# Pooled attention and two MLPs on one core: k's and v's rows loaded two tiles to a transfer, a batch's transfers ahead of its sums

## The chip, the core and the metric

The kernel runs on one core of one Trainium2 chip. A core has TensorE (PE: matrix products, with the loading of its stationary operand shown as PEld), VectorE (DVE), ScalarE (ACT), GpSimd (POOL), and SyncE (SP), whose queue here issues nearly all transfers; 16 DMA engines move the data. Each engine works through a queue of its own in the order of the program and waits at semaphores for the others. The metric is the device time of one execution in microseconds. Lower is better.

## What is computed

```python
def attn(q, k, v):            # (8, 8, 576, 64) each: batch, head, token, dim
    k_p = k.reshape(B, H, 72, 8, D).mean(axis=3)      # 72 pooled keys
    v_p = v.reshape(B, H, 72, 8, D).mean(axis=3)
    s = (q @ k_p.transpose(0, 1, 3, 2)) / sqrt(D)
    e = exp(s - s.max(-1)); return (e / e.sum(-1)) @ v_p
x = attn(q, k, v)             # as (4608, 512)
x = ((x @ w1) * (x @ w2)) @ w3 @ w_out                # w1, w2: 512 x 1024
out = relu(x @ w_in) ** 2 @ w_out2                    # 512 -> 2048 -> 512
```

## The kernel before

Every float32 operand of a large product is kept as two words, hi (ScalarE casts it) and lo (VectorE subtracts; `split`, L119 and L120), and a product is three matmuls: hi hi, hi lo, lo hi (`mm3`). In what follows, the cut of a tile is the VectorE instruction that makes its lo word. A matmul of 512 columns takes about 0.23 us.

The first 110 us are the start-up: `fold` multiplies w3 into w_out (L778), with the attention of the first tokens between. Then the 4608 tokens run as nine blocks of 512. A block has eight steps of `stage_ab` (24 matmuls ps_w, from x and w1 and w2; their product is gf, and its words are gt) and of `stage_w` (12 matmuls acc, from gt). The weights of half of these steps are fetched in units of 128x512 (`fetch`, L225, tile un, a ring of eight), each after TensorE has used the unit whose place it takes. After the nine blocks the second MLP runs over pairs of blocks with seven products in place of eight (`h_step`, L1088; `o_step`, L1190), the last block alone.

The attention that yields the next tokens is cut into tasks, and so is the preparation of the second MLP's weights ("quarters": tiles rq or raw, wq, sq, oq, stores u_A, u_S, u_oA, u_oS). Both are spread through the matmuls by `tick`, which `run_mm` calls after every six matmuls. Attention's tasks for a half of a batch's tokens are: the transposes of the pooled keys (ps_kt, copied to kbd), the scores (ps_s), their maxima on VectorE (mx, L467), the exponentials on ScalarE (att, L470) and sums (sm), transposes (ps_t; copied as aT, and the remainder as aR), four products with v (ps_av, first with aT, then with aR), and the casts and cuts that make x (L531, L534).

The pooling is the part that is changed. `kv_parts` loads a batch's k as five tiles (four of 128 rows, one of 64; every row is eight tokens of 64) and v as four tiles and a remainder ("odd", two transfers of 16 rows), 256 KB for a full tile, into the pool raw_p. The pool has three places, which it shares with the quarters' tiles rq and raw and later x2r. VectorE sums each tile over the eight tokens (`total`, L314, into kp or vp; the remainder of v, L311); v is then cut into vl and vr (L348). For every batch but the first, `load_back` takes one part from a list at each tick: part j sums tile j - 2 and issues the load of tile j. While a quarter is held between its loading and its conversion (`held`), no part is taken unless more than nine are left. The first batch's loads all go out at the beginning but for the last of v's tiles and the remainder, which a task of their own loads.

The operands of the next pair of blocks (`operands_of`: one load and seven cuts; x2r, x2o) are made in the steps h and o of the pair before it, at places that are written out by hand.

Of the kernel before, what the change touches and what calls it, by code (L numbers as in the profile page):

```python
# [35 lines left out]
def attn_moe_moe2_kernel(  # L36
# [242 lines left out]
    def load_back():  # L279
        if back["kv"] and not wait_kv[0] and (not held[0] or len(back["kv"]) > 9):  # L280
            back["kv"].pop(0)[1]()
        if back["q"] and ticks[0] % 2 == 0 and not (keep_q[0] and len(back["q"]) % Q_PARTS == 0):
            back["q"].pop(0)[1]()
# [3 lines left out]
    def kv_parts(src, b, dst, last):  # L287
# [4 lines left out]
        def load(j):  # L292
            pool, tag = (raw_p, "raw") if b else (wW_p, "w")
            if src is v and j == NP:
                raws[j] = r = pool.tile([RB, 2, POOL, D], F32, tag=tag, name="kv")
# [6 lines left out]
            raws[j] = r = pool.tile([P, POOL, D], F32, tag=tag, name="kv")  # L302
            if src is k:
                n = kv_rows(j)
                nc.sync.dma_start(r[:n], flat[j * P:j * P + n])
            else:
                nc.sync.dma_start(r, flat[j * 2 * SP:j * 2 * SP + P])

        def total(j):
            if src is v and j == NP:  # L310
                nc.vector.reduce_sum(v5, raws[j].rearrange("p a r d -> p a d r"), axis=AX.X)  # L311
                return
            n = kv_rows(j)
            nc.vector.reduce_sum(  # L314
                dst(j)[:n], raws[j][:n].rearrange("p r d -> p d r"), axis=AX.X)

        def part(j):
            if j >= 2:
                total(j - 2)
            if j < NJ:  # L320
                load(j)

        if b == 0:
            fits = NJ if src is k else U1 - NJ
            for j in range(fits):
                load(j)
            rest = [lambda: [load(j) for j in range(fits, NJ)]]
            return rest + [(lambda j=j: total(j)) for j in range(NJ)] + last
        parts = [(lambda j=j: part(j)) for j in range(NJ + 2)] + last
# [1077 lines left out]
    for step in order:  # L1407
        if step[0] == "h":
# [7 lines left out]
            if u == 0 and n == 0:  # L1416
                assert not todo_x
                head = False
            if u == NU - 1 and n in (1, 3, 4, 5, 6) and todo_x:
                todo_x.pop(0)()  # L1420
                head = n == 6
        elif step[0] == "ph":
            ph_step(*step[1:])
            prepare()
        else:
# [8 lines left out]
            if todo_x and head and step[2:] in ((0, 2), (0, 5), (1, 1), (1, 3)):  # L1434
# [36 lines left out]
```

## Time and profile before

| What | Value |
|---|---|
| time, median of 3 runs | 1528.61 us (1528.12 to 1530.61) |
| the profiled execution | 1530.13 us, of which the span shown is 1528.4 |
| TensorE busy | 1489.2 us, 97% of the span |
| VectorE, ScalarE busy | 997.0 us (65%), 797.2 us (52%) |
| mean granted clock of TensorE | 0.996 |
| transfers of k and v in full tiles | 32 each, 256 KB |

TensorE's busy share is the first thing to read: at 97% some 39 us are left in which it stands idle. About half of them lie in the start-up. The time of a whole run is a little longer than the span of the profile, which goes from the first to the last instruction.

### The profile page before, as it was taken

The page shows a single profiled execution, that of the slowest core. Times are in us where ns is not written, and L with a number is a line of the kernel's source. Part 1 is how long each engine was busy: PE and PEld are TensorE (multiplying, and loading weights), DVE is VectorE, ACT ScalarE, POOL GpSimd, SP SyncE. Part 2 cuts the span into 40 slices and gives each one's busy share as a digit, 9 for nine tenths or more (in the row PEclk, how much of TensorE's full clock was granted, in tenths as well). Part 3 has the DMA queues.
Part 4 walks back from the last instruction along what each step waited for, and adds up shares of the span by engine and source line. Part 5 has one row for each costly group of instructions (what it writes and reads, how often), then busy time and mean ns, then how long its engine had stood idle before and what let it go on. Part 6 is the DMA issues. An engine that isn't in the chain of part 4 may idle for free.

```text
span 1528.4 us, 21325 instructions
## 1 busy us (share of the span) xinstructions
PE 1489.2 (97%) x6752; PEld 1198.1 (78%) x6752; DVE 997.0 (65%) x1798; ACT 797.2 (52%) x1953; POOL 84.0 (5%) x144
## 2 busy tenths in 40 slices
PE   6899999999999999999999999999999999999998
PEld 3457778787888888878888878888888888888887
DVE  7998676757676368783255476759675967576542
ACT  6966464545545345563144574457445744464441
POOL 1011111111110011110000000000000000000000
PEclk9999999999999999999999999999999999999999
DMA  9555565757587257693339777777777867788752
GB/s 303 182 162 159 150 199 142 225 133 222 148 238 210 82 145 228 194 296 115 108 127 306 216 208 227 208 208 231 234 207 207 232 207 207 206 270 282 210 161 91
DMA packets 292783, 301.34 MB, mean 197 GB/s; under 512 B 119360, under 2 KB 184896, under 8 KB 292672
## 3 DMA queue, kind: packets, MB, share of 16 engines
q1 hardware_dynamic: 287488, 290.54, 65.3%
q10 hardware_dynamic: 5184, 9.44, 1.7%
q8 instruction: 55, 0.90, 0.3%
q14 instruction: 56, 0.46, 0.1%
HBM read 243.27 MB, written 56.62 MB: 196 GB/s over the span
## 4 chain that ended last, share of the span: by engine, by line
PE 70%; DVE 5%; ACT 3%; DMA 2%; issue 1%; SPq 0%; ACTq 0%; DVEq 0%
PE o L1190 18%; PE ps_w L185 17%; PE acc L185 8%; PE ps_a L1088 5%; PE ps_c L1088 5%; PE ps_d L1088 5%; PE ps_h L185 3%; PE o L185 3%; PE ps_b L1088 3%; PE ps_s L453 1%; PE ps_av L185 1%; ACT att L470 1%; DVE gt L120 1%; DVE x2o L120 1%; PE ps_t L500 1%
## 5 line engine op out<-in xcount | busy, mean ns | idle before, releaser
L1190 PE MATMUL o<-gt,un 128*128 128x512 f32 x1344 | 329.9, 390 | 1.4 <-DVE gt L120 1.0
L1190 PEld LDWEIGHTS o<-gt,un 128*128 128x128 f32 x1344 | 251.7, 188 | 56.0 <-DVE gt L120 3.5
L120 DVE TENSOR_TENSOR gt<-gs,gt 128x512 fp32r<-128x512 f32 x240 | 164.7, 688 | 182.9 <-ACT gt L119 181.5
L185 PE MATMUL ps_w<-x,wt 128*128 128x512 f32 x960 | 244.4, 400 | 4.4 <-ACT x L531 2.6
L119 ACT CAST gt<-gs 128x512 fp32r<-128x512 f32 x240 | 148.6, 620 | 154.7 <-PE o L1190 88.7
L185 PE MATMUL acc<-gt,Wt 128*128 128x512 f32 x864 | 215.9, 395 | 0.0
L185 PEld LDWEIGHTS ps_w<-x,wt 128*128 128x128 f32 x960 | 176.9, 190 | 44.0 <-DVE x L534 5.4
L185 PEld LDWEIGHTS acc<-gt,Wt 128*128 128x128 f32 x864 | 160.2, 188 | 32.3 <-issue 0.2
L185 PE MATMUL ps_w<-x,un 128*128 128x512 f32 x768 | 184.2, 392 | 0.0
L185 PEld LDWEIGHTS ps_w<-x,un 128*128 128x128 f32 x768 | 142.6, 188 | 29.6 <-issue 0.4
L470 ACT ACTIVATE att<-ps_s,mx 128x72 f32<-128x72 f32 (+1 forms) x320 | 97.8, 323 | 47.2 <-DVE mx L468 46.0
L1095 ACT ACTIVATE r<-r 128x512 f32<-128x512 f32 x96 | 60.7, 632 | 118.1 <-DVE r L1125 117.6
L815 DVE TENSOR_TENSOR gf<-asb,ps_w 128x512 f32<-128x512 f32 x72 | 49.3, 685 | 92.3 <-PE ps_w L185 85.4
L1088 PE MATMUL ps_a<-x2o,un 128*128 128x512 f32 x384 | 97.9, 389 | 0.2 <-ACT p L1113 0.2
L1088 PE MATMUL ps_c<-x2o,un 128*128 128x512 f32 x384 | 97.6, 389 | 0.0
L1088 PE MATMUL ps_d<-x2o,un 128*128 128x512 f32 x384 | 97.4, 389 | 0.0
L1096 ACT ACTIVATE gs<-r 128x512 f32<-128x512 f32 x144 | 90.0, 629 | 2.3 <-DMA x2r<-x2d 0.6
L1164 DVE TENSOR_TENSOR gs<-gs 128x512 f32<-128x512 f32 x128 | 86.6, 684 | 0.0
L119 ACT CAST gt<-gf 128x512 fp32r<-128x512 f32 x72 | 44.7, 621 | 79.2 <-DVE gf L815 79.2
L811 ACT COPY asb<-ps_w 128x512 f32<-128x512 f32 x72 | 42.3, 588 | 82.4 <-PE ps_w L185 82.0
L1088 PEld LDWEIGHTS ps_a<-x2o,un 128*128 128x128 f32 x384 | 72.0, 188 | 15.5 <-ACT p L1113 0.6
L1088 PEld LDWEIGHTS ps_c<-x2o,un 128*128 128x128 f32 x384 | 72.0, 188 | 15.2 <-DVE u L1119 0.3
(113 smaller groups left out, 1996.5 us busy)
## 6 DMA issues: line engine op xcount, KB each, us to landing
un<-u_w SPq DMA_DIRECT2D x128, 256.0 KB, 3.3
un<-u_A SPq DMA_DIRECT2D x128, 256.0 KB, 3.0
un<-u_S SPq DMA_DIRECT2D x128, 256.0 KB, 3.0
un<-u_oS SPq DMA_DIRECT2D x128, 256.0 KB, 3.0
un<-u_oA SPq DMA_DIRECT2D x96, 256.0 KB, 3.0
raw<-in_moe_w_dram SPq DMA_DIRECT2D x32, 512.0 KB, 5.4
raw<-in_moe_w_out_dram SPq DMA_DIRECT2D x24, 512.0 KB, 5.5
kv<-in_k_dram SPq DMA_DIRECT2D x32, 256.0 KB, 3.4
```

The source lines that it names most:

```text
L119: nc.scalar.copy(hi, src)
L120: return (eng or nc.vector).tensor_sub(lo, src, f32(hi))
L185: (lambda a=a, b=b, i=i: nc.tensor.matmul(ps, a, b, start=first and i == 0, stop=last and i == n - 1))
L453: nc.tensor.matmul(ps[:n, x * 2 * SP:(x + 1) * 2 * SP], t[:, hp, c0:c0 + n], kbd[:, hp].rearrange("p a s -> p (a s)"), start=True, stop=True)
L470: nc.scalar.activation(av[:, h0 + h], sv[:, h], ACTF.Exp, bias=mx[:n, h:h + 1], scale=scale, accum_out=sm[:n, h0 + h:h0 + h + 1])
L811: nc.scalar.copy(asb, ps)
L815: nc.vector.tensor_mul(gf, asb, pss[1])
L1088: nc.tensor.matmul(ps, l, r, start=first and j == 0, stop=j == len(todo) - 1, skip_group_check=True)
L1095: nc.scalar.activation(t, src, ACTF.Relu)
L1096: nc.scalar.activation(take(name), t, ACTF.Square)
L1164: d = nc.vector.tensor_sub(src, a, src)
L1190: nc.tensor.matmul(ob[x][o], l, r, start=u == 0 and m != 5 and j == 0, stop=u == NU - 1 and j == 2, skip_group_check=True)
```

## The change

k's and v's tiles are loaded two to a transfer: tiles 0 and 1, tiles 2 and 3, then the last one (or v's remainder). In the list of parts a batch's three loads come first, at three successive ticks, and then the sums, one to a tick: a tile that was summed two ticks after its load is now summed three to five ticks after it. The threshold of a held quarter goes from nine to ten parts. In the first batch k is loaded as before, and v's loads, remainder and all, are issued at the beginning; the two tasks that loaded the rest are gone. For the first pair of blocks, the cuts of the next pair's operands are taken at three places of the last h steps in place of five, at three o steps, and one in the next pair's second h step.

```diff
@@ -277,7 +277,7 @@
             back[name].pop(0)[1]()
 
     def load_back():
-        if back["kv"] and not wait_kv[0] and (not held[0] or len(back["kv"]) > 9):
+        if back["kv"] and not wait_kv[0] and (not held[0] or len(back["kv"]) > 10):
             back["kv"].pop(0)[1]()
         if back["q"] and ticks[0] % 2 == 0 and not (keep_q[0] and len(back["q"]) % Q_PARTS == 0):
             back["q"].pop(0)[1]()
@@ -289,44 +289,40 @@
         flat = src[b].rearrange("h (s r) d -> (h s) r d", r=POOL)
         raws = {}
 
-        def load(j):
-            pool, tag = (raw_p, "raw") if b else (wW_p, "w")
-            if src is v and j == NP:
-                raws[j] = r = pool.tile([RB, 2, POOL, D], F32, tag=tag, name="kv")
+        pool, tag = (raw_p, "raw") if b else (wW_p, "w")
+        groups = [[j] for j in range(NJ)] if src is k and b == 0 else [[0, 1], [2, 3], [4]]
+
+        def load(js):
+            if src is v and js == [NP]:
+                r = pool.tile([RB, 2, POOL, D], F32, tag=tag, name="kv")
+                raws[NP] = r.rearrange("p a r d -> p a d r")
                 odd = flat.rearrange("(a b s) r d -> b s a (r d)", a=2, b=2)
                 for x in range(2):
                     nc.sync.dma_start(
                         r[x * RM:(x + 1) * RM].rearrange("p a r d -> p a (r d)"),
                         odd[x, P:2 * SP])
                 return
-            raws[j] = r = pool.tile([P, POOL, D], F32, tag=tag, name="kv")
-            if src is k:
-                n = kv_rows(j)
-                nc.sync.dma_start(r[:n], flat[j * P:j * P + n])
-            else:
-                nc.sync.dma_start(r, flat[j * 2 * SP:j * 2 * SP + P])
+            m = len(js)
+            j0, n = js[0], kv_rows(js[0])
+            r = pool.tile([P, m, POOL, D], F32, tag=tag, name="kv")
+            rows_of = flat[j0 * P:j0 * P + n * m].rearrange(
+                "(j p) r d -> p j (r d)", j=m) if src is k else flat.rearrange(
+                    "(j w) r d -> w j (r d)", w=2 * SP)[:P, j0:j0 + m]
+            nc.sync.dma_start(r[:n].rearrange("p j r d -> p j (r d)"), rows_of)
+            for x, j in enumerate(js):
+                raws[j] = r[:n, x].rearrange("p r d -> p d r")
 
         def total(j):
-            if src is v and j == NP:
-                nc.vector.reduce_sum(v5, raws[j].rearrange("p a r d -> p a d r"), axis=AX.X)
-                return
             n = kv_rows(j)
             nc.vector.reduce_sum(
-                dst(j)[:n], raws[j][:n].rearrange("p r d -> p d r"), axis=AX.X)
-
-        def part(j):
-            if j >= 2:
-                total(j - 2)
-            if j < NJ:
-                load(j)
-
+                v5 if src is v and j == NP else dst(j)[:n], raws[j], axis=AX.X)
+
+        totals = [(lambda j=j: total(j)) for j in range(NJ)] + last
         if b == 0:
-            fits = NJ if src is k else U1 - NJ
-            for j in range(fits):
-                load(j)
-            rest = [lambda: [load(j) for j in range(fits, NJ)]]
-            return rest + [(lambda j=j: total(j)) for j in range(NJ)] + last
-        parts = [(lambda j=j: part(j)) for j in range(NJ + 2)] + last
+            for js in groups:
+                load(js)
+            return totals
+        parts = [(lambda js=js: load(js)) for js in groups] + totals
         what = (src is k, b)
         back["kv"].extend((what, fn) for fn in parts)
 
@@ -1414,11 +1410,14 @@
                 todo_x = operands_of(nxt) if nxt < len(pairs) else plain_operands()
                 todo_x.pop(0)()
             if u == 0 and n == 0:
-                assert not todo_x
+                assert len(todo_x) <= (p == 1)
                 head = False
-            if u == NU - 1 and n in (1, 3, 4, 5, 6) and todo_x:
+            if u == NU - 1 and n in ((1, 4, 6) if p == 0 else (1, 3, 4, 5, 6)) and todo_x:
                 todo_x.pop(0)()
                 head = n == 6
+            if p == 1 and u == 0 and n == 1:
+                todo_x.pop(0)()
+                assert not todo_x
         elif step[0] == "ph":
             ph_step(*step[1:])
             prepare()
@@ -1431,7 +1430,8 @@
                     sums_o.insert(0, t.rearrange("p x c -> p (x c)"))
             prepare()
             n_out += 1
-            if todo_x and head and step[2:] in ((0, 2), (0, 5), (1, 1), (1, 3)):
+            if todo_x and head and step[2:] in (
+                    ((0, 2), (0, 5), (1, 1)) if step[1] == 0 else ((0, 2), (0, 5), (1, 1), (1, 3))):
                 todo_x.pop(0)()
             (o_step if step[0] == "o" else po_step)(*step[1:])
     for p in reversed(late):
```

What stands in the queues before and now, at two places. In a row stand the line, the operation, and out<-in by the program's names. Tile numbers count differently in the two programs, and lines of the changed kernel are up to four lower (L467 is L463, L534 is L530) or, for the sums, L317.

VectorE in block 1, before: from v's fourth sum (vp) to the remainder's sum (v_99).

```order
L314 TENSOR_REDUCE vp<-kv 128x64
L467 TENSOR_REDUCE mx<-ps_s 128x4 x2
L468 TENSOR_SCALAR mx<-mx 128x4
L348 SCALAR_TENSOR_TENSOR vl<-vp,rows,vl 128x4x64
L468 TENSOR_SCALAR mx<-mx 128x4
L348 SCALAR_TENSOR_TENSOR vl<-vp,rows,vl 128x4x64
L815 TENSOR_TENSOR gf<-asb,ps_w_2073 128x512
L888 TENSOR_TENSOR sq<-wq,sq 128x256
L311 TENSOR_REDUCE v_99<-kv 32x128
L476 TENSOR_SCALAR sm<-sm 128x8
L120 TENSOR_TENSOR gt<-gf,gt 128x512
```

And now, from v's second sum to the maxima mx of the same scores:

```order
L317 TENSOR_REDUCE vp<-kv 128x64
L504 TENSOR_TENSOR aR<-ps_t,aR 32x2x128
L317 TENSOR_REDUCE vp<-kv 128x64 x2
L317 TENSOR_REDUCE v_99<-kv 32x128
L344 SCALAR_TENSOR_TENSOR vl<-vp,rows,vl 128x4x64 x2
L344 SCALAR_TENSOR_TENSOR vr<-v_99,rows,vr 32x2x64
L883 TENSOR_TENSOR sq<-wq 128x256
L463 TENSOR_REDUCE mx<-ps_s 128x4 x2
L464 TENSOR_SCALAR mx<-mx 128x4
L344 SCALAR_TENSOR_TENSOR vr<-v_99,rows,vr 32x2x64
L464 TENSOR_SCALAR mx<-mx 128x4
```

The remainder's sum and the cuts vl and vr stand ahead of the two maxima now; they stood behind them. TensorE at the same place, before, from the scores ps_s whose maxima these are:

```order
L453 MATMUL ps_s<-kbd,qT 128x144 x4
L185 MATMUL ps_w_2073<-x_2_883,wt 128x512 x3
L185 MATMUL ps_w_2073<-x_3_908,wt 128x512 x3
L185 MATMUL acc_1318<-gt,Wt 128x512 x3
L185 MATMUL acc_1319<-gt,Wt 128x512 x3
L500 MATMUL ps_t<-ident,att_105 128x128 x4
L185 MATMUL acc_1320<-gt,Wt 128x512
L505 MATMUL ps_t<-ident,rem 96x128 x2
```

And now:

```order
L449 MATMUL ps_s<-kbd,qT 128x144 x4
L185 MATMUL ps_w_2048<-x_2_861,wt 128x512 x3
L185 MATMUL ps_w_2048<-x_3_878,wt 128x512 x3
L185 MATMUL acc_1335<-gt,Wt 128x512 x3
L185 MATMUL acc_1336<-gt,Wt 128x512 x3
L185 MATMUL acc_1337<-gt,Wt 128x512 x3
L185 MATMUL acc_1338<-gt,Wt 128x512 x3
L496 MATMUL ps_t<-ident,att_105 128x128 x4
L501 MATMUL ps_t<-ident,rem 96x128 x2
```

The transposes ps_t stand behind twelve acc matmuls now, and stood behind six.

VectorE at the start of block 3, before:

```order
L815 TENSOR_TENSOR gf<-asb,ps_w_3611 128x512
L120 TENSOR_TENSOR gt<-gf,gt 128x512
L902 TENSOR_TENSOR oq<-sq,oq 128x512
L508 TENSOR_TENSOR aR<-ps_t,aR 32x2x64
L467 TENSOR_REDUCE mx<-ps_s 128x4
L468 TENSOR_SCALAR mx<-mx 128x4
L534 TENSOR_TENSOR x_0_2809<-ps_av,x_0_2809 128x64
L534 TENSOR_TENSOR x_0_3687<-ps_av,x_0_3687 128x256
L467 TENSOR_REDUCE mx<-ps_s 128x4
L314 TENSOR_REDUCE vp<-kv 128x64
```

And now:

```order
L811 TENSOR_TENSOR gf<-asb,ps_w_3545 128x512
L472 TENSOR_SCALAR sm<-sm 128x8
L473 RECIPROCAL sm<-sm 128x8
L120 TENSOR_TENSOR gt<-gf,gt 128x512
L317 TENSOR_REDUCE vp<-kv 128x64 x2
L504 TENSOR_TENSOR aR<-ps_t,aR 32x2x64
L463 TENSOR_REDUCE mx<-ps_s 128x4
L464 TENSOR_SCALAR mx<-mx 128x4
L317 TENSOR_REDUCE vp<-kv 128x64 x2
L530 TENSOR_TENSOR x_0_2772<-ps_av,x_0_2772 128x64
```

Two sums of v stand ahead of aR, and two more ahead of the first cut of x; none stood ahead of either. SyncE ahead of that, before, from the second of four unit fetches to the first loads of v:

```order
L225 DMA un<-u_w_5_1_1499 128x512
L209 DMA u_A_3_3223<-oq 128x2x128
L209 DMA u_A_2_3225<-oq 128x2x128
L209 DMA u_A_3_3227<-oq 128x2x128
L225 DMA un<-u_w_5_0_1375 128x512
L209 DMA u_A_2_3269<-oq 128x2x128
L225 DMA un<-u_w_5_1_1537 128x512
L209 DMA u_A_3_3271<-oq 128x2x128
L209 DMA u_A_2_3273<-oq 128x2x128
L209 DMA u_A_3_3275<-oq 128x2x128
L307 DMA kv<-in_v_dram 128x512 x3
```

And now, from two stores ahead of the second fetch to the last of v's loads:

```order
L209 DMA u_A_3_3279<-oq 128x2x128
L209 DMA u_A_2_3281<-oq 128x2x128
L225 DMA un<-u_w_5_1_1497 128x512
L209 DMA u_A_3_3283<-oq 128x2x128
L225 DMA un<-u_w_5_0_1377 128x512
L311 DMA kv<-in_v_dram 128x2x512
L225 DMA un<-u_w_5_1_1548 128x512
L311 DMA kv<-in_v_dram 128x2x512
L301 DMA kv<-in_v_dram 16x2x512 x2
```

v's first load stands behind the third fetch of the four now; it stood behind the fourth and three stores more.

## Rows read from the trace of the kernel before

**Rows 1.** Waits of TensorE: line, releaser, total, times, longest, in us.

```profile
PE ps_w L185 <- ACT x L531: 2.6, 1, 2.6
...
PE ps_t L500 <- DVE gf L815: 2.2, 1, 2.2
...
PE ps_w L185 <- DVE x L534: 1.7, 1, 1.7
...
PE o L1190 <- DVE gt L120: 1.0, 1, 1.0
```

**Rows 2.** Windows: length, busy PE, PEld, DVE, ACT, POOL, granted clock, DMA share, GB/s.

```profile
212.00:216.00 4.00, 2.28 (x11) 1.85 (x12) 4.00 (x8) 4.00 (x20) 0.00 (x0) 0.91 0.89 268
216.00:220.00 4.00, 4.00 (x13) 3.10 (x13) 1.25 (x4) 1.26 (x3) 1.62 (x3) 0.67 0.89 285
283.00:287.00 4.00, 3.77 (x16) 2.61 (x17) 3.88 (x11) 1.40 (x4) 1.15 (x1) 1.00 0.79 247
```

**Rows 3.** Timeline of TensorE in block 1: start, busy, instruction.

```profile
209.61 1.54 PE L185 MATMUL acc<-gt,Wt 128*128 128x512 f32 x6
213.37 0.63 PE L500 MATMUL ps_t<-ident,att 128*128 128x128 f32 x4 [2.22 <-DVE gf L815]
```

**Rows 4.** Timeline of VectorE in block 1.

```profile
198.98 0.46 DVE L467 TENSOR_REDUCE mx<-ps_s 128x4 f32<-128x288 f32 x1 [0.77 <-PE ps_s L453]
...
210.94 0.82 DVE L467 TENSOR_REDUCE mx<-ps_s 128x4 f32<-128x288 f32 x2
```

**Rows 5.** Groups of VectorE, 199 to 210.9: busy and mean.

```profile
L314 DVE TENSOR_REDUCE vp<-kv 128x64 f32<-128x512 f32 x4 | 4.1, 1056 | 0.0
L902 DVE TENSOR_TENSOR oq<-wq,oq 128x512 fp32r<-128x512 f32 x2 | 2.3, 1161 | 0.0
```

**Rows 6.** Window 199 to 211, VectorE's instructions on the tile rq alone.

```profile
199.00:211.00 12.00, 1.81 (x3) 1.00 0.57 175
```

**Rows 7.** Timeline of VectorE in the start-up.

```profile
27.43 0.17 DVE L476 TENSOR_SCALAR sm<-sm 128x8 f32<-128x8 f32 x1 [2.58 <-ACT att L470]
...
49.21 1.91 DVE L311 TENSOR_REDUCE v<-kv 32x128 f32<-32x1024 f32 x1
...
51.65 0.86 DVE L348 SCALAR_TENSOR_TENSOR vl<-vp,rows,vl 128x256 fp32r<-128x256 f32 x2
```

**Rows 8.** DMA view: issues, count, KB each, median us to landing.

```profile
raw<-in_moe_w_out_dram SPq DMA_DIRECT2D x24, 512.0 KB, 5.5
...
kv<-in_v_dram SPq DMA_DIRECT2D x32, 256.0 KB, 4.0
...
x2r<-x2d SPq DMA_DIRECT2D x2, 512.0 KB, 4.8
```

**Rows 9.** All transfers of the tile kv.

```profile
DMA to landing us min/median/max: 2.1/3.4/8.6
```

**Rows 10.** Timeline of TensorE at the start of block 2.

```profile
268.24 5.60 PE L185 MATMUL ps_w<-x,un 128*128 128x512 f32 x24
...
277.00 0.66 PE L453 MATMUL ps_s<-kbd,qT 128*128 128x144 f32 x4
```

**Rows 11.** Timeline of VectorE there.

```profile
273.95 0.69 DVE L815 TENSOR_TENSOR gf<-asb,ps_w 128x512 f32<-128x512 f32 x1 [2.12 <-PE ps_w L185]
```

**Rows 12.** Timeline of TensorE at the start of block 3.

```profile
353.71 3.04 PE L185 MATMUL ps_w<-x,un 128*128 128x512 f32 x12
...
361.03 0.30 PE L518 MATMUL ps_av<-aR,vr 96*128 96x320 f32 x1
```

**Rows 13.** Timeline of VectorE there.

```profile
358.75 0.69 DVE L120 TENSOR_TENSOR gt<-gf,gt 128x512 fp32r<-128x512 f32 x1 [0.69 <-ACT gt L119]
```

**Rows 14.** Timeline of SyncE there.

```profile
355.90 0.42 SPq L225 DMA_DIRECT2D un<-u_w  x1
```

**Rows 15.** Timeline of ScalarE in block 7.

```profile
677.27 0.62 ACT L898 CAST oq<-sq 128x512 fp32r<-128x512 f32 x1 [1.88 <-DMA u_oA<-oq]
```

**Rows 16.** Timeline of VectorE in the last half-steps of the first pair.

```profile
903.44 1.90 DVE L120 TENSOR_TENSOR x2o<-x2r,x2o 128x512 fp32r<-128x512 f32 x3
```

## The prediction

> **What bounds the kernel now.** I read the waits of TensorE first: it is busy 97% of the span, so little but its own gaps can change the time. After the start-up only four gaps exceed half a microsecond: 2.6, 2.2, 1.7 and 1.0 us, each once [rows 1]. Before them stands the start-up (folding w3 into w_out), whose idle time is spread over many short waits.
>
> A gap costs more than its length. After the 2.2 us gap the granted clock is 0.91 in the stretch of the gap and 0.67 in the next: between the chip's two levels, 2.4 GHz (1.00) and 1.2 GHz (0.50). After the 1.7 us gap it stayed at 1.00 [rows 2]. I take the loss behind a long gap as (1 - 0.67) x 4 us = 1.3, plus some of the 0.36 of the stretch before: 1.5 us.
>
> So the change is worth what it does to these gaps, less the gaps that it opens. It lives on VectorE's queue, which works in the order of the program: a sum of v that stands there and waits for its transfer holds every cut behind it.
>
> **Block 1 (the 2.2 us gap).** The reader sees TensorE end its acc matmuls at 211.1 and wait for ps_t until 213.37 [rows 3]. What it lacks are exponentials whose maxima VectorE took only at 210.94, after working without a pause from 198.98 [rows 4]: 2.4 us from the maxima to ps_t. In the new order three conversions of rq stand earlier and leave this stretch (1.81 us, [rows 6]) and so does one cut oq (1.16, [rows 5]): 3.0 us. The remainder of v (1.91) comes in, with two cuts vl (0.86) and a smaller one, vr (my estimate 0.3) [rows 7]: 3.1 us. The maxima stay at about 210.9, ps_t at 213.3. But TensorE now has twelve acc matmuls ahead of ps_t, not six: 1.5 us more work [rows 3], so it arrives at 212.5 and waits 0.8 to 0.9. Gain 2.2 - 0.9 = 1.3, and without the fall of the clock 1.5 more: **-2.8**. Bounds: 0 (the wait stays) and -3.7 (it goes).
>
> **Block 2 (the 1.7 us gap).** New: the first pair of v tiles is issued one unit fetch and one store into the 24 matmuls that begin at 268.24. A fetch waits for six matmuls, a quarter of 5.60: 269.6; two issues at 0.4 [rows 14] put the transfer at 270.5 [rows 10]. How long 512 KB of k or v take, no row shows. The nearest rows: 4.0 for 256 KB of v, 4.8 and 5.5 for 512 KB of other tensors [rows 8]; 3.4 is the median of kv's own transfers and 8.6 their longest [rows 9]. I take 4.8, the row of like size whose 512 KB stand alone; bounds 3.4 and 8.6. It lands at 275.3. VectorE is there at 274.6, after gf [rows 11], and now has the two sums (1.06 each, [rows 5]) ahead of gt: 277.4; gt 278.1, a third sum 279.1, x's cut 279.5. TensorE reaches the matmul that needs this cut after ps_s (277.00 and 0.5) and three more at 0.23: 278.4 [rows 10]. It waits 1.1 in place of 1.7: **-0.5**. At 3.4 the wait is 0.5 (-1.2); at 8.6 it is 4.9 and the clock falls (+4.7).
>
> **Block 3 (no gap now).** The same move opens one. Now aR's cut follows oq, and the sums come much later. New: two sums stand ahead of aR. The transfer follows the third fetch, which needs the first six of twelve matmuls from 353.71: 355.2 [rows 12], issued at 355.6 (as late as 356.3 if the fetch comes at 355.90 as now, [rows 14]); landing 360.4. VectorE is free at 359.4 [rows 13], waits, sums until 362.5, cuts aR at 362.8. TensorE now reaches aR's matmul at 361.03 [rows 12]; four more acc matmuls stand ahead of it, so 361.9. Wait 0.9. Then two more sums stand ahead of x's cut: maxima until 363.4, sums until 365.5, cut 365.8, against TensorE's arrival at 365.1 (five acc's, ps_s and one matmul after aR): 0.7. Behind these two cuts TensorE's next acc and ps_w matmuls are queued, and no other engine. **+1.6**, no fall of the clock since each gap is under 1.7. At 3.4: aR is in time and only the 0.7 is left (+0.7); at 8.6: 4.7 + 0.7 + 1.5 = +6.9.
>
> At one place a rule and the rows differ. The rows give 4.8 and 5.5 for 512 KB [rows 8]. The Trainium skill (DMA: Bandwidth & Descriptors, section Anatomy of one DMA) gives a transfer a fixed 2.0 us and its bytes at 436 GB/s, fitted on another issuing path; my estimate by that page is 3.2 us for 512 KB, and the sum would be that of the third case below. No transfer of 512 KB in these rows is so fast.
>
> **The other parts.** Sums of k go four in one piece in block 2; TensorE's ps_s waits a little for the copy behind them: **+0.2** (0 to 0.8). Blocks 4 to 6: the maxima stand ahead of the sums in the new order, and TensorE has twelve or more ps_w matmuls of an older block to fill: 0, as it is now; without that fill they would cost what block 3 does. Block 7 (2.6 us): x's cast waits behind an oq cast that a store's landing released [rows 15]. Its quarter runs one step earlier now, but two wq conversions come ahead of the cast: **-0.3** (-4 to +1).
>
> The first pair: three operand cuts stand before gt (1.90 us for three, [rows 16]). In the new order three instructions fewer precede the same gt, 1.9 us, more than the 1.0 of the gap: **-1.0** (0 to -1.0). The cuts themselves move behind the gt's, under o matmuls that do not wait for them.
>
> The start-up: all of v's first sums now come in one go, before the first aT. That is one sum, the remainder and three cuts moved ahead: 1.06 + 1.91 + 0.86 + 0.6 = 4.4 us [rows 5, 7], into a place where VectorE sat idle for 2.58 [rows 7]. The work behind it is 1.8 late, but 4.4 us go from the middle of the fold, where TensorE waits for the same engine. Bounded by -2.6 (the idle time is all won) and +1.8 (only the delay counts); I take **-1.0**. DMA issues become fewer everywhere: of k five per batch become three, of v six become four.
>
> **The sum.** -2.8 - 0.5 + 1.6 + 0.2 - 0.3 - 1.0 - 1.0 = -3.8. The profiled execution took 1530.1 us, 1.5 more than the median of the runs (1528.61): 1526.3 for such an execution, 1524.8 for the median.
>
> **Rivals.**
> First, slower: the pairs of transfers land late. Both go out back to back, 1 MB beside fetches and stores; 8.6 us has been seen [rows 9]. Block 3's sums then hold aR. At a landing of 8 us: block 2 +4.1, block 3 +6.3, sum +5.5, 1534.1. It decides from 6.8 us on (sum above +3). Against it: 4.8 and 5.5 for like sizes.
> Second, no change: block 1's wait stays, since VectorE still takes the maxima last. Then the first term is 0, the sum -1.0, 1527.6. For it: the maxima do not move in my own count.
> Third, faster than forecast: transfers issued earlier are landed when their sums come. At 3.4 us block 2 gives -1.2, block 3 +0.7, k 0: sum -5.6, 1523.0. For it: 3.4 is kv's median. This is the case of the Trainium skill's advice (the same page, Rules for kernel authors) to issue a transfer early and wait for it late.
>
> **Chances.** Forecast 0.38 (its own range 1522.5 to 1527), third 0.20, second 0.24, first 0.18. A measurement of this kernel tells about 0.2%, 3.06 us, from no change. Of the forecast's 0.38, 0.25 lie beyond that: faster 0.25 + 0.20 = 0.45; same 0.13 + 0.23 = 0.36; slower 0.19. The range 1520.5 to 1533 leaves out the farther halves of the first and third cases.
>
> **What would show it.** Right: ps_t's wait in block 1 below 1.2 us and the clock at 1.00 behind it; waits near 1 us on x's cut in block 2 and on aR and x in block 3; the gap before o gone; 512 KB of kv landing in 4 to 5.5 us. Wrong: a wait above 2 us with a lower clock at block 3, the 2.2 us wait of block 1 unmoved, or a start-up that ends over 2 us earlier or later than now, since its order on TensorE changes at many places and I have counted only VectorE's.

## The result and the profile after

The change made the kernel slower: 1538.93 us (1535.36 to 1540.09, 6 runs) against 1528.36 us of before on the same chip (1526.96 to 1531.37, 6 runs), a ratio of 1.0058 [1.0046, 1.0071]. Forecast were 1524.8 us, within 1520.5 to 1533, and a small gain. A second set of runs on another chip, below, gave 1.0036. The profiled execution after took 1535.36 us, its span 1533.6. It is the fastest of the six: its span is 5.2 us longer than that of before, while 0.58% are 8.9 us. Where the other 3.7 go, no trace here shows.

The waits of TensorE after, the answer to [rows 1] (line, releaser, total, times, longest, in us):

```profile
PE ps_t L496 <- issue: 4.3, 5, 1.3
PE ps_w L185 <- ACT x L527: 3.4, 2, 2.1
PE ps_t L501 <- DVE aT L120: 3.2, 2, 1.9
PE ps_w L774 <- DVE wo L155: 2.9, 2, 2.4
...
PE ps_av L185 <- DVE x L530: 2.4, 1, 2.4
PE ps_w L185 <- DVE x L530: 1.6, 2, 1.0
PE ps_s L449 <- ACT att L466: 1.5, 1, 1.5
...
PE ps_av L185 <- DVE aR L504: 0.8, 1, 0.8
```

The gaps of 2.2 and 1.0 us are gone, those of 2.6 and 1.7 are 2.1 and 1.0. But others have come: 2.4 (on wo), 2.4 (on x) and 1.9 us (on aT) in the start-up, 1.5 in block 0, 1.3 and 0.8 in later blocks.

**The start-up.** TensorE after, from the transposes of the second aT (start, busy, instruction):

```profile
30.84 0.63 PE L501 MATMUL ps_t<-ident,rem 128*96 128x128 f32 x2 [1.88 <-DVE aT L120]
31.26 2.85 PE L399 MATMUL ps_q<-ident,q_nat 128*128 128x128 f32 x12
34.17 2.29 PE L449 MATMUL ps_s<-kbd,qT 128*128 128x144 f32 x8
38.91 8.07 PE L774 MATMUL ps_w<-wo,w3t 128*128 128x512 f32 x12 [2.44 <-DVE wo L155]
```

And before, where the twelve matmuls of the fold stood ahead of the scores ps_s:

```profile
31.41 6.86 PE L778 MATMUL ps_w<-wo,w3t 128*128 128x512 f32 x12 [0.41 <-DVE wo L155]
...
38.54 0.90 PE L453 MATMUL ps_s<-kbd,qT 128*128 128x144 f32 x6
```

VectorE after, at that place: it sits idle until the scores come, and the steps that make wo follow their maxima.

```profile
35.54 0.46 DVE L463 TENSOR_REDUCE mx<-ps_s 128x4 f32<-128x288 f32 x1 [2.71 <-PE ps_s L449]
36.50 0.46 DVE L463 TENSOR_REDUCE mx<-ps_s 128x4 f32<-128x288 f32 x1 [0.50 <-PE ps_s L449]
36.87 0.42 DVE L152 TENSOR_SCALAR raw<-raw 128x512 uint32<-128x512 uint32 x1
```

In the windows after (columns as in [rows 2]) the clock stays at its lower level nearly throughout:

```profile
30.00:33.00 3.00, 2.11 (x9) 1.73 (x10) 1.95 (x5) 2.79 (x12) 1.40 (x3) 0.61 1.03 412
33.00:36.00 3.00, 2.94 (x14) 2.42 (x13) 0.46 (x1) 2.65 (x6) 0.22 (x2) 0.50 0.29 116
36.00:39.00 3.00, 0.56 (x3) 0.24 (x2) 2.47 (x7) 2.25 (x8) 0.00 (x0) 0.50 0.01 3
39.00:42.00 3.00, 3.00 (x4) 1.38 (x5) 2.86 (x6) 3.00 (x12) 0.00 (x0) 0.50 0.64 188
42.00:45.00 3.00, 3.00 (x5) 1.14 (x4) 2.93 (x7) 1.93 (x7) 0.00 (x0) 0.61 0.73 203
```

Before, two of these windows were below 1.00:

```profile
30.00:33.00 3.00, 2.60 (x10) 1.53 (x11) 2.90 (x5) 3.00 (x7) 0.00 (x0) 0.66 0.46 164
33.00:36.00 3.00, 3.00 (x7) 1.25 (x6) 2.97 (x7) 2.80 (x5) 0.00 (x0) 0.77 0.83 264
```

A window's time at 1.2 GHz is 2 x (1 - clock) x its length: 13.7 us after, 3.4 before. It fell behind waits of 0.9 and 1.9 us between 27.5 and 30.9 us, and the gap of 2.44 lies in the middle of it.

From the fold's first product to its last, before and after:

```profile
15.36:111.67 96.31, 83.92 (x311) 44.54 (x311) 90.38 (x177) 74.23 (x206) 11.19 (x17) 0.98 0.66 207
```

```profile
16.77:116.60 99.83, 87.92 (x315) 48.32 (x316) 88.46 (x178) 75.94 (x214) 10.66 (x17) 0.91 0.66 200
```

TensorE is idle for 12.4 us of this stretch before and 11.9 after, so its waits have not grown in sum; the 3.5 us more are time in which it is busy, at a clock of 0.91 in place of 0.98.

**The blocks.** TensorE after, at the places of the prediction (block 1, 2, 3) and at two more:

```profile
215.34 2.90 PE L185 MATMUL acc<-gt,Wt 128*128 128x512 f32 x12
219.50 0.63 PE L496 MATMUL ps_t<-ident,att 128*128 128x128 f32 x4 [1.25 <-issue]
220.71 0.39 PE L501 MATMUL ps_t<-ident,rem 128*96 128x128 f32 x2 [0.58 <-issue]
...
283.64 0.50 PE L185 MATMUL ps_w<-x,wt 128*128 128x512 f32 x1 [1.04 <-DVE x L530]
...
364.87 0.70 PE L185 MATMUL ps_av<-aT,vl 128*128 128x320 f32 x3 [0.83 <-DVE aR L504]
...
606.31 2.62 PE L185 MATMUL ps_w<-x,wt 128*128 128x512 f32 x9 [1.29 <-ACT x L527]
...
907.09 16.48 PE L1186 MATMUL o<-gt,un 128*128 128x512 f32 x72
```

Block 1: twelve acc matmuls stand ahead of ps_t and the wait is 1.25 in place of 2.2 [rows 3]; the granted clock from 216 to 220 us is 1.00. Blocks 2 and 3: waits of 1.04 and 0.83. At 907 the o matmuls run without a gap.

**Where the time went.** Waits hide each other, so I also took from each profile the start of fixed matmuls: the fold's first product, the 1st and the 145th acc matmul (the second is in block 1), the first and the last o matmul. In the last column stands the span:

| kernel | fold's first | first acc | 145th acc | first o | last o | span |
|---|---|---|---|---|---|---|
| before | 15.4 | 134.4 | 265.4 | 900.3 | 1479.8 | 1528.4 |
| after | 16.8 | 141.1 | 267.5 | 907.1 | 1485.2 | 1533.6 |
| after minus before | +1.4 | +6.6 | +2.1 | +6.8 | +5.4 | +5.2 |

From the fold's first product to the first acc 5.2 us are lost (3.5 up to the fold's last product, 1.7 behind it, in block 0), block 1 gives 4.5 back, blocks 2 to 8 lose 4.7, the first pair gives back 1.4. The first 1.4 us, ahead of the fold, are no work of the change: the kernels that leave the first batch alone vary there from 15.4 to 17.4.

### The profile page after: what moved, and what is told of

Read it like the earlier page. It is cut to its first block, busy times and chain, and to the rows that moved or that the text cites. A ratio compares the mean times of both kernels' runs of the same rounds, so it can differ in the third digit from the quotient of the medians.

```text
span 1533.6 us, 21274 instructions
## 1 busy us (share of the span) xinstructions
PE 1490.1 (97%) x6752; PEld 1201.4 (78%) x6752; DVE 994.3 (65%) x1798; ACT 798.6 (52%) x1953; POOL 83.3 (5%) x144
## 4 chain that ended last, share of the span: by engine, by line
PE 83%; DVE 7%; DMA 4%; ACT 3%; issue 2%; SPq 1%; DVEq 0%; ACTq 0%
PE ps_w L185 22%; PE o L1186 18%; PE acc L185 11%; PE ps_c L1084 5%; PE ps_a L1084 5%; PE ps_d L1084 5%; PE ps_h L185 3%; PE o L185 3%; PE ps_b L1084 3%; PE ps_s L449 2%; PE ps_w L774 2%; PE ps_av L185 1%; DMA raw<-in_moe_w_out_dram 1%; DMA raw<-in_moe_w_dram 1%; PE ps_t L496 1%
## 5 line engine op out<-in xcount | busy, mean ns | idle before, releaser
L811 DVE TENSOR_TENSOR gf<-asb,ps_w 128x512 f32<-128x512 f32 x72 | 49.3, 684 | 99.6 <-PE ps_w L185 94.5
L1084 PEld LDWEIGHTS ps_d<-x2o,un 128*128 128x128 f32 x384 | 72.1, 188 | 15.0
```

Of the source, the lines that this page charges most:

```text
L811: nc.vector.tensor_mul(gf, asb, pss[1])
L1084: nc.tensor.matmul(ps, l, r, start=first and j == 0, stop=j == len(todo) - 1, skip_group_check=True)
```

## The experiments

Each kernel ran beside the kernel before on the same chip; a ratio is to that, with its 95% interval. None leaves out a part of the computation.

### Which part costs the time

First the change in its parts. Alone in the first batch (the kernel before with this, and v's loads in pairs; k as before):

```diff
         if b == 0:
-            fits = NJ if src is k else U1 - NJ
-            for j in range(fits):
-                load(j)
-            rest = [lambda: [load(j) for j in range(fits, NJ)]]
-            return rest + [(lambda j=j: total(j)) for j in range(NJ)] + last
+            for js in groups:
+                load(js)
+            return totals
```

> The kernel before with the first batch alone changed: v's five transfers of the beginning in pairs, remainder with them, no task that loads the rest; later batches and the first pair as before. Theory A, the start-up costs (v's last sums and cuts stand ahead of the first aT, the fold's operands come later, TensorE idles and its clock falls at 30 to 44 us): 6 to 10 us slower than before, 1534 to 1539, with the fall of the clock in the start-up. Theory B, the pairs of transfers and the late sums of the later batches cost: within 1 us of before, 1528.

1531.3 us, **1.0007 [0.9995, 1.0019]**: not the 6 to 10 us of theory A. The later batches alone (the whole change of `load` and of the list, without the first batch's and the pair's part):

```diff
-        if back["kv"] and not wait_kv[0] and (not held[0] or len(back["kv"]) > 9):
+        if back["kv"] and not wait_kv[0] and (not held[0] or len(back["kv"]) > 10):
...
-        parts = [(lambda j=j: part(j)) for j in range(NJ + 2)] + last
+        parts = [(lambda js=js: load(js)) for js in groups] + totals
```

> The kernel before with only the later batches changed (loads in pairs and first, sums later, threshold ten). Theory A: TensorE's start-up as before; block 1 gains 2 to 3, blocks 2, 3 and 5 lose about as much: 1527 to 1529.5. Theory B: 6 to 10 us slower, 1534 to 1539.

1534.26 us, **1.0031 [1.0019, 1.0043]**. The changed kernel with the first batch as it was:

```diff
-        groups = [[j] for j in range(NJ)] if src is k and b == 0 else [[0, 1], [2, 3], [4]]
+        groups = [[j] for j in range(NJ)] if b == 0 else [[0, 1], [2, 3], [4]]
...
-            for js in groups:
+            fits = NJ if src is k else U1 - NJ
+            for js in groups[:fits]:
                 load(js)
-            return totals
+            rest = [lambda: [load(js) for js in groups[fits:]]]
+            return rest + totals
```

> The changed kernel with the first batch loaded as before. Theory A: what is left is only_later and the first pair's change, worth 1.0 to 1.4: 1526 to 1528.5. Theory B: 1535 to 1539, as the changed kernel.

1532.96 us, **1.0017 [1.0006, 1.0027]**, between the two ranges. And the changed kernel with the first pair's operands at their old places:

```diff
-            if u == NU - 1 and n in ((1, 4, 6) if p == 0 else (1, 3, 4, 5, 6)) and todo_x:
+            if u == NU - 1 and n in (1, 3, 4, 5, 6) and todo_x:
...
```

> The changed kernel with the first pair's operands at their old places. Theory A: the wait before the first pair's o matmuls is back at 1.0 us, 1.0 to 1.4 us slower than the changed kernel: 1536.5 to 1540.5. Rival C, the move of the operands itself costs: 3 us or more faster than the changed kernel, below 1536.

1538.52 us, **1.0069 [1.0051, 1.0087]**. So the later batches cost 0.3%; the first batch alone costs nothing that can be told, though its start-up has the same long fall of the clock (0.53, three times 0.50 and 0.69 in the five windows above). Its profile loses 1.6 us from the fold to the first acc and 3.6 in blocks 2 to 8, and gains 5.3 between. My first theory, that the start-up is the cause, fell here. The parts do not explain the whole, either: the first batch and the later ones together, as in this last kernel, cost 0.69%, alone 0.07 and 0.31, all on one chip.

### The start-up and the list's empty places

The first batch's change also takes two places out of the list of tasks: one that is empty for k, and the one that loaded the rest of v. Without them in the kernel before:

```diff
-            rest = [lambda: [load(j) for j in range(fits, NJ)]]
-            return rest + [(lambda j=j: total(j)) for j in range(NJ)] + last
+
+            def lead():
+                [load(j) for j in range(fits, NJ)]
+                total(0)
+            return [lead] + [(lambda j=j: total(j)) for j in range(1, NJ)] + last
```

> The kernel before without the two empty places in the list of attention's tasks (k's empty load task, and v's load task joined to the first sum); all transfers as before. Theory A, refined: the wait of block 1 left the changed kernel because attention runs two tasks ahead, and the fall of the clock at 30 to 44 us came from v's early transfers alone. So here the start-up is that of before (one fall of 3.4 us), the 2.2 us wait for gf is gone and a wait of 1.3 us stands there without a fall: 1 to 3 us faster than before. Rival: the start-up's long fall comes from the places in the list too: 1 to 3 us slower than before.

1531.52 us, **1.0013 [1.0004, 1.0022]**: slower, as the rival had it, and not for its reason. Block 1's gap is gone and the start-up's fall is 3.4 us, both as theory A said, but the time did not follow. The first batch's change with both places put back:

```diff
-            return totals
+            return [lambda: None] + totals
```

> only_first with the two empty places put back. Theory A: the long fall of the clock in the start-up (13.65 us) is still there, and the 2.2 us wait of block 1 with its fall is back: 2 to 5 us slower than before, 1.5 to 3 slower than only_first. Rival: both follow the places in the list, and it takes the time of before.

1531.4 us, **1.0015 [1.0006, 1.0024]**: 2.3 us over before, within theory A's range. The first batch's change with the second half of q loaded ahead of v:

```diff
-        first_v = load_v(0)
         load_q(0, 1)
+        first_v = load_v(0)
```

> only_first with the second half of the first batch's q loaded ahead of v. The fold's next six products stand ahead of the scores in TensorE's queue again, as before. Theory A: the start-up's order costs, not the amount that is loaded: the fall of the clock at 30 us is 3.4 us or none, and the time is 2 to 4 us under only_first. Rival: the 0.33 MB more that are moved early cost: as only_first, within 1 us.

1530.99 us, **1.0009 [0.9999, 1.0018]**: as the first batch's change alone. Theory A fell: the fold's twelve matmuls stand ahead of the scores again, and the clock is 0.50 in three of the five windows above and 0.80 in the fourth all the same, behind waits of 2.1 and 2.0 us. And the places gone, with the pair's new places:

> before_slots_gone with the first pair's operands at the changed kernel's places. Theory A: the 1.0 us wait ahead of the first pair's o matmuls is gone: 1.0 to 1.4 us under before_slots_gone, 2 to 4 under before. If the two gains do not add: within 0.5 us of before_slots_gone.

1528.9 us, **0.9994 [0.9985, 1.0003]**, not the 2 to 4 us under before. TensorE in block 1 with the first batch's change, and then with the places put back:

```profile
211.27 2.90 PE L185 MATMUL acc<-gt,Wt 128*128 128x512 f32 x12
214.02 0.63 PE L503 MATMUL ps_t<-ident,att 128*128 128x128 f32 x4
```

```profile
214.89 1.54 PE L185 MATMUL acc<-gt,Wt 128*128 128x512 f32 x6
218.62 0.84 PE L503 MATMUL ps_t<-ident,att 128*128 128x128 f32 x4 [2.19 <-DVE gf L818]
```

The removed list places took block 1's gap away: twelve matmuls ahead of ps_t without them, six with them, and the old 2.2 us gap with them also in the later batches' part alone. It was not the later batches' loads and sums, from which I had still expected 2 to 3 us there when that part ran.

### What it is about the later batches

The later batches' part again, with the sums at their old ticks (base: the later batches alone):

```diff
+        def part(j):
+            if j >= 2:
+                total(j - 2)
+            if j < len(groups):
+                load(groups[j])
...
```

> only_later with the sums back at the ticks of before: transfers in pairs at three successive ticks, every tile summed two ticks after the first transfer as before, seven parts, threshold nine. Theory L, the lateness of the sums costs: the waits of 2.0 us at 118.9 and 2.1 us in block 3 are gone, within 1.5 us of before. Theory T, the transfers of two tiles cost (they land later, or crowd the fetches): 3 to 4.5 us slower than before, as only_later.

1533.95 us, **1.0030 [1.0020, 1.0040]**, as theory T said. Single tiles as before, with the sums a tick later (base: before):

```diff
-        if back["kv"] and not wait_kv[0] and (not held[0] or len(back["kv"]) > 9):
+        if back["kv"] and not wait_kv[0] and (not held[0] or len(back["kv"]) > 10):
...
-            if j >= 2:
-                total(j - 2)
+            if j >= 3:
+                total(j - 3)
...
```

> The kernel before with every sum of the later batches one tick later (three ticks after the first load, eight parts, threshold ten); transfers of one tile as before. Theory L: the waits of only_later stand here too, 3 to 4.5 us slower than before. Theory T: within 1.5 us of before.

1528.29 us, **0.9996 [0.9985, 1.0006]**. With these two ran the changed kernel once more, and the kernel before with the pair's new places alone:

> The changed kernel once more, beside the others on one chip. If the parts add, it takes before plus 0.7 (first batch) plus 3.7 (later batches) less 1.3 (first pair), 3 us slower; if they do not, 8 to 10 us slower as before, and the profile shows in which stage TensorE waits or its clock falls where neither part alone has it.

1535.47 us, **1.0036 [1.0022, 1.0051]**, between the two cases.

> The kernel before with the first pair's operands at the changed kernel's places and nothing else. Theory: the 1.0 us wait ahead of the first pair's o matmuls goes and nothing else moves: 1.0 to 2.6 us faster than before, the best of the kernels run. Rival, the cuts moved into the second pair wait or hold something there: no faster.

1530.47 us, **1.0004 [0.9994, 1.0015]**: no gain that can be told, against my 1.0 to 2.6 us. The lateness of the sums is not the cause of the whole: late sums of single tiles cost nothing that can be told, early sums of tiles of two cost as much as late ones. So it is the tiles of two: their transfer, or something else about them. First the transfer: each tile of two filled by two transfers of 256 KB, with the later batches alone and in the changed kernel:

```diff
-            nc.sync.dma_start(r[:n].rearrange("p j r d -> p j (r d)"), rows_of)
+            for x in range(m):
+                nc.sync.dma_start(r[:n, x:x + 1].rearrange("p j r d -> p j (r d)"), rows_of[:, x:x + 1])
```

> only_later with each tile of two filled by two transfers of 256 KB, issued one behind the other at the same place. Theory T1, a sum waits for the landing of its pair's second half: the wait of VectorE for v in block 3 falls from 2.9 us to under 1.9, and the time is within 1.5 us of before. Theory T2, the loads going out close together costs: 3 to 4.5 us slower than before, as only_later.

1535.31 us, **1.0034 [1.0021, 1.0046]**, as slow as theory T2 said.

> The changed kernel with each pair's transfer split in two, nothing else. Theory T1: 2.5 to 4 us faster than the changed kernel, which was 5.5 to 9 us slower than before: 1530.5 to 1534. Theory T2: as the changed kernel, 1534 to 1538.

1533.39 us, **1.0022 [1.0004, 1.0039]**. This lies where theory T1 had it, but the interval also takes in the 1.0036 of the changed kernel's second set: whether the split helps there is open. Then how close the loads stand: at the first, third and fifth tick, again on both.

```diff
-        parts = [(lambda js=js: load(js)) for js in groups] + totals
+
+        def part(j):
+            if j >= 3:
+                total(j - 3)
+            if j % 2 == 0 and j < 2 * len(groups):
+                load(groups[j // 2])
```

> only_later with a batch's three loads at the first, third and fifth tick in place of three successive ones; sums at the same ticks. Theory T2, the loads' closeness costs: the 512 KB of raw that block 6 waits for land in under 6 us in place of 7.2, and the time is within 1.5 us of before. Theory T3, the tiles of two cost wherever they are loaded: 3 to 5 us slower than before, as only_later and pairs_split.

1536.79 us, **1.0040 [1.0025, 1.0055]**. The 512 KB of raw landed in 6.7 us, not in under 6.

> The changed kernel with its three loads at the first, third and fifth tick. Theory T2: 3 to 5 us faster than the changed kernel, 1530 to 1533. Theory T3: as the changed kernel, 1534 to 1538.

1535.22 us, **1.0030 [1.0018, 1.0042]**, both as slow as theory T3 said or slower. For the later batches alone neither smaller transfers nor loads further apart won anything back. In block 3 VectorE's wait for v's first sum was 2.9 us with the later batches alone, 1.2 with split and 0.7 with spread transfers, and the times did not follow.

Where the tiles of two lose, two kernels with the same sums at the same ticks show best: the later batches alone, and single tiles with late sums. VectorE in block 0, tiles of two:

```profile
115.05 1.02 DVE L317 TENSOR_REDUCE kp<-kv 128x64 f32<-128x512 f32 x1
...
117.96 1.94 DVE L317 TENSOR_REDUCE kp<-kv 128x64 f32<-128x512 f32 x2
...
119.89 1.03 DVE L317 TENSOR_REDUCE kp<-kv 64x64 f32<-64x512 f32 x1
...
120.96 0.76 DVE L465 TENSOR_REDUCE mx<-ps_s 128x4 f32<-128x288 f32 x2
```

And single tiles with late sums:

```profile
118.24 0.45 DVE L467 TENSOR_REDUCE mx<-ps_s 128x4 f32<-128x288 f32 x1
...
118.92 0.40 DVE L467 TENSOR_REDUCE mx<-ps_s 128x4 f32<-128x288 f32 x1
119.24 1.08 DVE L314 TENSOR_REDUCE kp<-kv 128x64 f32<-128x512 f32 x1
...
120.30 1.07 DVE L314 TENSOR_REDUCE kp<-kv 64x64 f32<-64x512 f32 x1
```

With tiles of two all sums of k stand ahead of these maxima; with single tiles the last two stand behind them. Up to 112 us the two kernels are level (TensorE's first ps_w matmuls start at 112.35 and 112.21). Then TensorE waits for exponentials, first with tiles of two:

```profile
118.92 1.33 PE L451 MATMUL ps_s<-kbd,qT 128*128 128x144 f32 x4 [2.02 <-ACT att L468]
```

```profile
117.98 0.76 PE L453 MATMUL ps_s<-kbd,qT 128*128 128x144 f32 x4 [1.41 <-ACT att L470]
```

In the window from 117 to 121 us TensorE is busy 2.08 us at a clock of 0.67 with the first, and 3.02 at 1.00 with the second:

```profile
117.00:121.00 4.00, 2.08 (x7) 1.89 (x8) 4.00 (x9) 1.80 (x9) 0.40 (x1) 0.67 0.44 139
```

```profile
117.00:121.00 4.00, 3.02 (x15) 2.59 (x16) 3.97 (x11) 3.23 (x19) 1.78 (x4) 1.00 0.57 189
```

The order of the sums is not enough to explain this. Tiles of two with early sums have all sums of k ahead of the same maxima too, and a wait of 0.66:

```profile
118.82 1.08 DVE L317 TENSOR_REDUCE kp<-kv 64x64 f32<-64x512 f32 x1
...
119.92 0.78 DVE L472 TENSOR_REDUCE mx<-ps_s 128x4 f32<-128x288 f32 x2
```

```profile
117.81 0.76 PE L458 MATMUL ps_s<-kbd,qT 128*128 128x144 f32 x4 [0.66 <-ACT att L475]
```

From the fold's last product to the first acc they take 23.1 us; the five kernels with single tiles and the list's places take 22.4 to 22.9, the four others with tiles of two and the places 24.9 to 26.5. So in block 0 tiles of two cost with late sums; in blocks 2 to 8, below, with early ones too.

In block 6 the quarter's raw lands 7.2 us after its issue with tiles of two and 5.4 with single tiles, and holds ScalarE for 1.9 and 0.4 us, x's casts behind it.

The last kernel puts together what had cost nothing or gained: single tiles, sums a tick later, and the pair's new places.

> single_sums_late (single tiles, sums one tick later) with the first pair's operands at the changed kernel's places. If the 1.0 us gap of the first pair is worth its length: 1.0 to 1.5 us faster than before. If it isn't: within 0.7 us of before.

1527.65 us, **0.9988 [0.9980, 0.9997]**, the only one whose interval lies below the kernel before, and by little for one of 17; its mean granted clock is 0.998.

### All profiles together

The stretches between the fixed matmuls of above, as means over the profiles with single tiles or tiles of two, and with the list's places kept or gone (19 profiles: those of the 17 runs above, the first of the changed kernel, and that of before):

| mean, us | profiles | fold's first to first acc | to 145th acc | blocks 2 to 8, to first o |
|---|---|---|---|---|
| single tiles, places kept | 5 | 119.1 | 131.0 | 633.6 (631.7 to 635.0) |
| single tiles, places gone | 4 | 122.0 | 126.0 | 637.1 (636.4 to 638.5) |
| tiles of two, places kept | 5 | 120.4 | 130.6 | 638.1 (637.4 to 640.1) |
| tiles of two, places gone | 5 | 123.4 | 126.3 | 640.3 (636.9 to 643.8) |

Tiles of two cost 1.3 us ahead of the first acc, with the places kept and gone, and 4.5 and 3.2 us in blocks 2 to 8. With the middle column (-0.4, +0.3) that is 5.4 and 4.8 us, or 0.36 and 0.31%: what the runs of the later batches show. With the places kept the two ranges of the last column do not meet; with the places gone they do. Without the list's two places the stretch to the 145th acc is 4.9 and 4.3 us shorter, but the start-up 2.9 and 3.0 longer and blocks 2 to 8 3.5 and 2.1: together +1.5 and +0.8. Block 1's gain is real and is given back. From the first to the last o matmul the eleven profiles with the pair's old places took 579.5 to 579.7 us, the eight with the new ones 578.1 or 578.2.

## Why the prediction was wrong

The sum was -3.8 and the span grew by 5.2, 9.0 us more. By the stretches above, 1.4 of the 9.0 lie ahead of the fold and are not the change's. From the fold's first product to the first acc I had -1.0 and it became +5.2; block 1 gave 4.5 where I had 2.8; for blocks 2 to 8 I had +1.0 and they lost 4.7; the first pair gave 1.4 where I had 1.0. So two steps failed: the start-up, and the places in the blocks that I had put at nothing.

**Block 1 (-2.8): mechanism right, size off.** TensorE did come later, behind twelve acc matmuls, and waited 1.25 us (I had 0.8 to 0.9) at a full clock. The stretch to the 145th acc matmul became 4.5 us shorter. But the cause was the removed list places, and I did not ask what else these shift: the start-up takes back 3 us, blocks 2 to 8 the rest and more.

**Block 2 (-0.5): the number right, by luck.** x's cut waits 1.04, where I had 1.1. But I had VectorE wait for the first pair of tiles and the third sum follow at once. The first pair was there in time; it was the third sum that waited for the second pair:

```profile
282.38 1.01 DVE L317 TENSOR_REDUCE vp<-kv 128x64 f32<-128x512 f32 x1 [1.05 <-DMA kv<-in_v_dram]
```

A second wait of 0.5 on x's cuts I did not have. **Block 3 (+1.6): half right.** aR waits 0.83 (I had 0.9), the 0.7 on x is absent. The transfer was issued at 357.42 and VectorE's sum could begin at 362.49, which makes 5.1 us for issue and landing against my 4.8. VectorE waited only 0.17 of it, where I had 1.0: it was late itself, with gt ahead of the sums.

```profile
362.49 2.01 DVE L317 TENSOR_REDUCE vp<-kv 128x64 f32<-128x512 f32 x2 [0.17 <-DMA kv<-in_v_dram]
```

**Blocks 4 to 6 (0), and block 0, which had no term: a failed step.** I followed the sums only where the kernel before had its gaps or the new order a plain delay, and put the rest at nothing. The waits after are 1.46 and 1.22 in block 0 and 1.29 in block 6. With tiles of two blocks 2 to 8 are 3.2 to 4.5 us longer on average, and the stretch ahead of the first acc 1.3. My terms for blocks 2 to 8 (-0.5, +1.6, +0.2 and -0.3) came to +1.0, for block 0 to nothing.

**Block 7 (-0.3): about right.** x's cast waits 2.1 in place of 2.6, and 1.34 on an aT elsewhere in the block.

**The first pair (-1.0): right.** The gap is gone, the stretch from the first to the last o matmul 1.4 us shorter in every profile that has the new places. The runs alone are too coarse to tell it: the new places in the kernel before gave 1.0004 [0.9994, 1.0015].

**The start-up (-1.0, bounds -2.6 to +1.8): the other failed step.** Up to the fold's last product it is 3.5 us longer, beyond my bound and the sign of being wrong that I had named, and the stretch to the first acc 5.2 (124.3 against 119.1). Of the 5.2 the means give 3.0 to the list places and 1.3 to the tiles of two, whose loss lies in block 0; I had neither. What I did price, v's earlier loads, I saw on VectorE's queue alone. On TensorE's they bring the scores ahead of the fold's twelve matmuls, the steps that make wo fall behind the scores' maxima, and the clock falls for long. That order is not the whole reason: with q loaded ahead of v it is as before, and the clock fell too. I had the idle time change and the clock stay; the idle time stayed and the clock fell. That costs time: six profiles share the first batch's change (the changed kernel's two, those with split and spread loads, with the pair's old places, and the first batch alone), and their fold takes 97.0 us with 9.7 us at the lower level, 97.7 and 97.7 with 13.7, 99.6 with 17.9, 99.8 with 18.0 and 100.8 with 20.2, by estimate 0.36 us for each us at that level (the times at it come from the mean clock of the stretch, given to 0.01, and are good to 1 us). Whether v's earlier loads cost anything in sum is not settled. With the list places gone and single tiles, the two kernels with these loads took 120.7 and 122.5 us to the first acc and the two without 123.1 and 121.8; with the places kept, the one with them took 121.9 and the four without 116.8 to 119.4.

**The rivals.** The second, that block 1's wait stays, fell: it halved. The first, slower, foretold the right side for another reason. Its condition, a landing of v's pairs past 6.8 us, did not occur where I had put it, nor in the median: 512 KB took a median of 5.3 us for v and 4.1 for k, answering [rows 8]:

```profile
kv<-in_v_dram SPq DMA_DIRECT2D x16, 512.0 KB, 5.3
```

and splitting the transfers did not help the later batches. By the Trainium skill (DMA: Bandwidth & Descriptors, Anatomy of one DMA) my estimate had been 3.2 us; the measurement decides against it. The third rival fell with that: no landing was near its 3.4 us in the median, and in block 3 aR waited although the transfer was only 0.17 us late. The same page's Rules for kernel authors advise to coalesce many small transfers into one large; no run here gained by it, and for the later batches the loss stayed when each pair was split again into two transfers.

**What stays open.** Why tiles of two cost about 5 us is not settled. What the traces suggest: the pool has three places, so with single tiles the loads of a batch's last tiles wait for a place until the first sums are done, and the last sums come late in VectorE's queue, between the maxima, as in block 0 above. With tiles of two a whole batch fits, and its sums stand in one bunch ahead of them. This is argued, not shown, and early sums speak against it in block 0. A rival is that the quarters share the three places: a batch of tiles of two takes all of them, and a quarter's load of rq waits. In the later batches alone these loads (L923) wait in SyncE's queue for kv's landings and sums:

```profile
SPq L923 <- DMA kv<-in_v_dram: 9.6, 3, 4.1
SPq L923 <- DVE kp L317: 7.0, 2, 4.4
```

With vp's 3.1 that is 19.7 us in all; with single tiles and late sums it is 3.1 for v and vp together. No run separates the two; more places in the pool, for single tiles and for tiles of two, would. Nor is it settled why the whole change cost 0.36% on one chip and 0.58% on the other, where its parts add to 0.29% (0.07 and 0.31, less 0.09, the mean of four differences with and without the pair's places: -0.14, -0.19, -0.08, +0.04).

## What to carry to other kernels

Where TensorE is busy 97% and a change re-deals the queues, price it at every place where the moved work now stands ahead of something on the path, not only at the gaps that the kernel has: a gap that goes is counted against gaps that open. Before a coarser transfer is judged by how long it takes to land, ask what its tile's place in the pool does to the order of the work behind it and to the others that share the pool; here the traces only suggest that this is what cost. And remove empty entries of a task list with the same care as full ones: they set what stands ahead of what.

## What was unexpected of the hardware

TensorE was at its lower level for 13.7 us of the start-up after (worked out above) and for 3.4 before. In the second profile of the changed kernel the granted clock from 15 to 50 us was 0.85, in the first 0.80, so a rerun of the same program, here on another chip, can differ by 3.5 us at the lower level (2 x 0.05 x 35). The length of a fall is not the time lost, either: by the six profiles above a us at the lower level went with 0.36 us more in the fold, and the first batch's change alone has the long fall while its runs, with block 1's gain, are at 1.0007. And two transfers of 256 KB into one tile landed v in a median of 4.7 us each, with single tiles and late sums it was 3.9 for the same size: in these runs a landing took longer where more was issued at once.
